# Linear attention and expert layer on one core: unit 0's sums of key exponentials moved from TensorE to GpSimd, with a new order of all instructions

## The chip, the cores and the metric

One core of a Trainium2 chip (trn2) runs the whole program. The metric is the device time of one execution in microseconds (us); of several runs the median is taken. Engines are named as in the profile: PE is TensorE, DVE is VectorE, ACT is ScalarE, POOL is GpSimd, SP is SyncE, from whose queue the transfers start. PEld are TensorE's weight loads.

## The reference

Attention over 8 batches of 8 heads, 576 tokens of 64 values each, and then a layer over the 4608 tokens, 512 wide with 1024 inner values:

```python
def phi(x):
    proj = np.einsum('bhsd,df->bhsf', x, w_phi)
    proj = proj - np.max(np.abs(proj), axis=-1, keepdims=True)
    return np.concatenate([np.exp(proj), np.exp(-proj)], axis=-1)
q_p, k_p = (phi(q), phi(k))
kv = np.einsum('bhsf,bhsd->bhfd', k_p, v)
z = np.sum(k_p, axis=2)
num = np.einsum('bhsf,bhfd->bhsd', q_p, kv)
den = np.einsum('bhsf,bhf->bhs', q_p, z)[..., None] + 1e-06
...
h = x @ w_in
e = np.exp(h - np.max(h, axis=-1, keepdims=True))
solu = h * (e / (np.sum(e, axis=-1, keepdims=True) + 1e-09))
ln = (solu - mu) / np.sqrt(var + 1e-06) * g_ln
out = ln @ w_out
```

The change concerns `z`, the sum of the key features over the tokens of one head.

## The kernel before

The attention is cut into 16 units, 0 to 15; unit u holds half the heads of batch u // 2, and two halves (sub 0 and sub 1) of two heads each. For each unit PE projects keys and queries (`pjk`, `pjq`, and `pjm` for the tokens in the middle), DVE takes the largest absolute value of a row (`m`) and subtracts it (`dk`, `dq`), ACT takes the exponentials (`ek` for keys, `fq` for queries). PE then multiplies key exponentials with values into `kvT` (`kv_mm`, and `kv_rest` for the tokens in the middle), adds `z` into the same bank, and later makes the numerator (`num`) and the denominator (`den`). The reciprocal of the denominator goes through a transfer that spreads it over rows (`rb<-d`), and POOL multiplies it into the result (`xa`, `xb`), which is the input of the second layer.

The second layer runs in 36 token tiles of 128: PE makes `h` with three products of high and low parts (`mxh`, `mxl`), DVE, ACT and POOL make the gated values, a transfer turns them, and PE makes `o`. A tile's `mxl` comes from POOL (`moe_lo`, line 1073). The last tile's `o` is made in two column halves (`moe_o_last`, line 1177), all others in one width of 512. Before the first `h`, the weights have to be unpacked: by ACT (`wraw`), by DVE (`wb`, two instructions a block), and by POOL (`win_l`, four blocks; `wsum`, the sums for the centring of `w_out`, whose mean PE makes as `cmall`).

There are two ways to the sums `z`. A unit in `Z_PE` takes them on PE (`z_mm`, line 613): for four token groups 16 products of the exponentials with ones, for the middle four more with `ones_half`, so 20 in each half. Every other unit has POOL add first: `z_add` (line 555) twice in each half, each with one addition of 128x512 into `zt` and one of 128x256 into `zacc`, and `z_half` (line 563), one of 64x512 for the middle. PE then needs four products with ones (`kv_z`, line 604). The choice stands in `z_sums`:

```python
def z_sums(st, sub):
    if st["u"] in Z_PE:
        z_mm(st, sub, list(key_tiles(st, sub)))
    else:
        kv_z(st, sub)
```

All instructions are steps of one plan (class `Plan`, line 211). The order in which they are written is the tuple `SEQUENCE` of step numbers (line 55), the same for all engines; each engine runs its own instructions in that order, and buffers are given to steps in that order too. `InOrder` (line 254 and after; its call is line 260, to which the profile puts nearly all instructions) keeps it.

Of the kernel before, what the change touches and what calls it, by code (L numbers as in the profile page):

```python
# [24 lines left out]
Z_PE = (0, 1, 2)  # L25
# [246 lines left out]
def linear_attention_then_moe(ctx, tc, qT, kT, v, w_phi, w_in, g_ln, w_out, out):  # L272
# [601 lines left out]
    for u in range(2 * B):  # L874
# [53 lines left out]
        for g in range(3):  # L928
            z = (0.0, 4.0, 6.0)[g]
            for j in (None,) if g == 1 else range(2):  # L930
# [3 lines left out]
                if g != 1 and u in K_BANKED:  # L934
# [4 lines left out]
                    src + [("e", g, j)])  # L939
        for sub in () if u in Z_PE else range(2):  # L940
            z, e = 1.5 + 4.5 * sub, 2 * sub
# [365 lines left out]
```

## Time and profile before

| what | value |
|---|---|
| median of 3 runs | 661.49 us (661.01 to 664.86) |
| profiled execution | 661.79 us |
| its span, first to last instruction | 659.8 us |
| PE busy | 652.9 us (99%), 4876 instructions |
| DVE busy | 503.9 us (76%) |
| POOL busy | 413.2 us (63%), 447 instructions |
| ACT busy | 373.5 us (57%) |
| granted PE clock | 1.0, full speed in every slice of the span |

The span is shorter than the execution by 1.99 us that lie around it. A busy share is a mean over the whole span; the first 68 us are the attention of units 0 to 2 and the preparation of the weights, and what follows is a mixture of attention and the second layer.

### The profile page before, as it was taken

How to read it: one execution, taken by the hardware profiler on the slowest of the kernel's cores; microseconds unless marked ns; L12 is line 12 of the kernel's file. 1: busy time of each engine (PE TensorE's matmuls, PEld its weight loads, DVE VectorE, ACT ScalarE, POOL GpSimd, SP SyncE). 2: the span in 40 equal slices, each digit the busy share in tenths (PEclk: the TensorE clock that was granted, in tenths of full speed). 3: DMA queues.
4: the chain of work that ended last, by engine and by line, in shares of the span. 5: the costliest groups of instructions: out<-in, count | busy, mean ns of one | idle time of the engine just before them, and what ended most of it. 6: DMA issues, size and time to landing. Idle time of an engine off the chain costs nothing.

```text
span 659.8 us, 13101 instructions
## 1 busy us (share of the span) xinstructions
PE 652.9 (99%) x4876; PEld 489.6 (74%) x4876; DVE 503.9 (76%) x756; ACT 373.5 (57%) x719; POOL 413.2 (63%) x447
## 2 busy tenths in 40 slices
PE   8999999999999999999999999999999999999998
PEld 7666767668777777777768777777777767888887
DVE  6999989899988789697878878688787945454530
ACT  4997875666555755556556555367366544323222
POOL 0249999867749578275773868738564955553632
PEclk9999999999999999999999999999999999999999
DMA  8978887587787668776777665886656372362342
GB/s 277 379 241 264 251 253 215 191 244 231 218 273 245 211 174 274 225 236 219 217 233 249 189 195 164 275 292 211 198 173 178 112 220 81 115 207 96 129 160 80
DMA packets 133296, 138.44 MB, mean 210 GB/s; under 512 B 55665, under 2 KB 106737, under 8 KB 132721
## 3 DMA queue, kind: packets, MB, share of 16 engines
q1 hardware_dynamic: 133232, 137.61, 66.6%
q8 instruction: 38, 0.62, 0.4%
q14 instruction: 26, 0.20, 0.1%
HBM read 87.10 MB, written 50.48 MB: 209 GB/s over the span
## 4 chain that ended last, share of the span: by engine, by line
PE 84%; POOL 5%; DVE 5%; DMA 3%; SPq 1%; issue 1%; ACT 1%; POOLq 0%; DVEq 0%
PE o L260 28%; PE h L260 27%; PE kvT L260 12%; PE num L260 6%; PE pjk L260 4%; PE pjq L260 4%; PE den L260 2%; DVE m L260 2%; POOL zt L260 1%; SPq L260 1%; POOL zacc L260 1%; DVE dk L260 1%; DMA rawk<-in_k 1%; PE pjm L260 1%; POOL w L260 1%; DVE dq L260 1%
## 5 line engine op out<-in xcount | busy, mean ns | idle before, releaser
L260 PE MATMUL o<-w_out_h,uhs 128*128 128x512 f32 (+1 forms) x296 | 114.3, 386 | 0.0
L260 PE MATMUL o<-w_out_l,uhs 128*128 128x512 f32 (+1 forms) x296 | 113.5, 383 | 0.0
L260 PE MATMUL o<-w_out_h,uls 128*128 128x512 f32 (+1 forms) x296 | 113.5, 383 | 0.0
L260 ACT ACTIVATE ek<-dk 128x512 f32<-128x512 f32 (+1 forms) x160 | 88.9, 587 | 32.3 <-DVE dk L260 20.1
L260 POOL TENSOR_TENSOR uls<-uTs,uhs 128x1024 fp32r<-128x1024 f32 x36 | 87.0, 2422 | 31.8 <-ACT uhs L260 31.6
L260 POOL TENSOR_TENSOR zt<-ek 128x512 f32<-128x512 f32 x52 | 68.6, 1320 | 54.4 <-ACT ek L260 41.9
L260 PE MATMUL h<-win_h,mxh 128*128 128x512 f32 x288 | 91.4, 399 | 0.1
L260 PE MATMUL h<-win_h,mxl 128*128 128x512 f32 x288 | 89.1, 391 | 0.2 <-POOL mxl L260 0.2
L260 PE MATMUL h<-win_l,mxh 128*128 128x512 f32 x288 | 89.0, 390 | 0.0
L260 ACT ACTIVATE fq<-pT 128x512 f32<-128x512 f32 (+1 forms) x140 | 74.2, 561 | 17.9 <-PE kvT L260 9.7
L260 DVE TENSOR_REDUCE nm<-h 128x1 f32<-128x1024 f32 x36 | 43.8, 1217 | 52.5 <-PE h L260 52.4
L260 ACT ACTIVATE eu<-h,nm 128x1024 f32<-128x1024 f32 x36 | 40.1, 1115 | 74.8 <-DVE nm L260 55.5
L260 PEld LDWEIGHTS o<-w_out_h,uhs 128*128 128x128 f32 x296 | 55.6, 188 | 12.1 <-issue 0.9
L260 PEld LDWEIGHTS o<-w_out_h,uls 128*128 128x128 f32 x296 | 55.6, 188 | 11.0
L260 PEld LDWEIGHTS o<-w_out_l,uhs 128*128 128x128 f32 x296 | 55.6, 188 | 10.7
L260 PEld LDWEIGHTS h<-win_h,mxl 128*128 128x128 f32 x288 | 53.8, 188 | 12.4 <-POOL mxl L260 1.1
L260 DVE SCALAR_TENSOR_TENSOR qz<-fq,kvf,qz 128x576 f32<-128x576 f32 x52 | 57.6, 1124 | 6.8 <-ACT qz L260 6.7
L260 PEld LDWEIGHTS h<-win_l,mxh 128*128 128x128 f32 x288 | 54.1, 188 | 11.6
L260 PEld LDWEIGHTS h<-win_h,mxh 128*128 128x128 f32 x288 | 52.3, 188 | 13.9 <-issue 1.6
L260 PE MATMUL kvT<-ek,rawv 128*64 128x256 f32 x512 | 61.6, 383 | 1.0 <-DVE dk L260 0.7
L260 POOL TENSOR_TENSOR xa<-E,rb 128x576 f32<-128x576 f32 (+1 forms) x32 | 30.4, 950 | 47.0 <-DMA rb<-d 46.5
L260 DVE TENSOR_TENSOR eu<-h,eu 128x1024 f32<-128x1024 f32 x36 | 43.6, 1211 | 19.5 <-ACT eu L260 19.3
(96 smaller groups left out, 1244.0 us busy)
## 6 DMA issues: line engine op xcount, KB each, us to landing
du<-ub SPq DMA_DIRECT2D x36, 512.0 KB, 3.9
uTs<-du SPq DMA_DIRECT2D x36, 512.0 KB, 4.6
rb<-d SPq DMA_DIRECT2D x64, 144.0 KB, 4.1
dqd<-dq SPq DMA_DIRECT2D x14, 640.0 KB, 4.2
pT<-dqd SPq DMA_DIRECT2D x14, 640.0 KB, 6.1
out<-os SPq DMA_DIRECT2D x35, 256.0 KB, 3.2
rawq<-in_q SPq DMA_DIRECT2D x32, 256.0 KB, 4.5
rawk<-in_k SPq DMA_DIRECT2D x32, 256.0 KB, 4.2
```

The costliest lines, as they stand in the source:

```text
L260: return self.tc.keep_in_program_order(method(*args, **kwargs))
```

## The change

`Z_PE` loses unit 0, so that unit 0's `z` takes the way of units 3 to 15: ten additions on POOL (two `z_add` and one `z_half` in each half) and four products in each half on PE in place of twenty. The number of steps grows by six, and `SEQUENCE` is another order from its first entries on; nothing else differs.

```diff
-Z_PE = (0, 1, 2)
+Z_PE = (1,2)
...
 SEQUENCE = (
-    123, 2, 1, 124, 125, 78, 87, 129, 127, 126, 80, 81, 135, 94, 83, 89, 128, 84, 104, 85, 136, 82, 102, 95,
...
```

On PE, in unit 0's part, from the middle products (`vz`) to the transposition of `kvT` (`kvt`), before:

```order
L260 MATMUL kvT<-ek,vz 64x256 x4
L260 MATMUL kvT<-ek,ones 32x128 x16
L260 MATMUL kvT<-ek,ones_half 32x128 x4
L260 MATMUL kvT<-ek,rawv 64x256 x8
L260 MATMUL kvT<-ek,ones 32x128 x16
L260 MATMUL kvT<-ek,ones_half 32x128 x4
L260 MATMUL kvt<-ident,kvs 128x128 x3
```

and now:

```order
L261 MATMUL kvT<-ek,vz 64x256 x4
L261 MATMUL kvT<-zacc,ones 32x128 x4
L261 MATMUL kvT<-ek,rawv 64x256 x8
L261 MATMUL kvT<-zacc,ones 32x128 x4
L261 MATMUL dT<-ident,dqm 128x128 x4
L261 MATMUL kvt<-ident,kvs 128x128 x6
```

Two times twenty products became two times four, which read what POOL adds, and the two transpositions of `kvT` moved together behind one of the queries.

On POOL, the first tensor instructions of the program, behind the constants, before:

```order
L260 TENSOR_TENSOR win_l<-w_0_472,win_h 128x1024
L260 TENSOR_TENSOR win_l<-w_1_433,win_h 128x1024
L260 TENSOR_TENSOR xa<-E,rb 128x576 x2
L260 TENSOR_TENSOR wsum<-w_4_613 128x512
L260 TENSOR_TENSOR wsum<-wsum,w_5_637 128x512 x2
```

and now, from the seventh of the ten additions on (`zt` and `zacc` are the additions for `z` of unit 0):

```order
L261 TENSOR_TENSOR zacc<-zacc,ek 64x512
L261 TENSOR_TENSOR zt<-ek 128x512
L261 TENSOR_TENSOR zacc<-zt 128x256
L261 TENSOR_TENSOR zacc<-zacc,ek 64x512
L261 TENSOR_TENSOR win_l<-w_0_495,win_h 128x1024
L261 TENSOR_TENSOR win_l<-w_1_448,win_h 128x1024
L261 TENSOR_TENSOR wsum<-w_4_540 128x512
L261 TENSOR_TENSOR xa<-E,rb 128x576
L261 TENSOR_TENSOR wsum<-wsum,w_5_599 128x512 x2
```

The ten additions stand ahead of everything else there, and the first sum for the centring (`wsum`, numbered 4) moved ahead of the first division (`xa`); the second division moved behind the sums.

On PE, from unit 2's last key products to the first `h` of the second layer, before:

```order
L260 MATMUL kvT<-ek,rawv 64x256 x8
L260 MATMUL kvT<-ek,ones 32x128 x16
L260 MATMUL kvT<-ek,ones_half 32x128 x4
L260 MATMUL cmall<-wsum,mean 128x512
L260 MATMUL pjk<-wph,rawk 128x128 x8
L260 MATMUL pjq<-wph,rawq 128x128 x8
L260 MATMUL pjm<-wph,rawk 128x128 x2
L260 MATMUL pjm<-wph,rawq 128x128 x2
L260 MATMUL h<-win_h,mxh 128x512 x2
```

and now:

```order
L261 MATMUL cmall<-wsum,mean 128x512
L261 MATMUL kvT<-ek,rawv 64x256 x8
L261 MATMUL kvT<-ek,ones 32x128 x16
L261 MATMUL kvT<-ek,ones_half 32x128 x4
L261 MATMUL pjk<-wph,rawk 128x128 x8
L261 MATMUL pjm<-wph,rawk 128x128 x2
L261 MATMUL pjm<-wph,rawq 128x128 x2
L261 MATMUL pjq<-wph,rawq 128x128 x8
L261 MATMUL h<-win_h,mxh 128x512 x2
```

The mean (`cmall`) moved ahead of unit 2's last key products. All PE steps that stood ahead of the first `h` still do, except one: `pjm` of unit 4 comes behind it now (the `pjm` shown is unit 3's, which stood earlier before).

At the end of the program ACT's last work (`eu` is the gated exponential, `uhs` the high part of a turned tile, `os` the eviction of `o`) was, before:

```order
L260 CAST uhs<-uTs 128x1024 x2
L260 ACTIVATE os<-o,sc 128x512
L260 CAST uhs<-uTs 128x1024
L260 ACTIVATE eu,sm<-h,nm 128x1024
L260 CAST uhs<-uTs 128x1024
L260 ACTIVATE os<-o,sc 128x512 x4
L260 ACTIVATE os<-o,sc 128x256 x2
```

and is now:

```order
L261 CAST uhs<-uTs 128x1024
L261 ACTIVATE eu,sm<-h,nm 128x1024
L261 ACTIVATE os<-o,sc 128x512 x3
L261 CAST uhs<-uTs 128x1024 x2
L261 ACTIVATE os<-o,sc 128x512
L261 ACTIVATE os<-o,sc 128x256 x2
L261 ACTIVATE os<-o,sc 128x512
```

The second half of tile 34's `o` is PE's last work now, behind both halves of tile 35, and so a tile of full width is the last to be evicted and written out.

## Rows read from the trace of the kernel before

**Rows 1.** Busy time by stretch: PE, PEld, DVE, ACT, POOL, PE clock, DMA share, GB/s.

```profile
13.00:42.00 29.00, 28.70 (x410) 20.41 (x408) 28.93 (x54) 27.13 (x53) 4.74 (x2) 1.00 0.92 328
42.00:68.00 26.00, 26.00 (x356) 17.57 (x353) 25.93 (x43) 20.20 (x41) 24.25 (x15) 1.00 0.83 266
68.00:330.00 262.00, 261.73 (x1978) 191.58 (x1976) 226.44 (x345) 164.84 (x327) 188.21 (x201) 1.00 0.76 230
330.00:630.00 300.00, 299.20 (x1907) 227.93 (x1906) 210.85 (x296) 148.61 (x282) 184.11 (x204) 1.00 0.59 184
```

**Rows 2.** Timeline of PE, unit 0, sub 1: start, duration, instructions.

```profile
21.10 1.08 PE L260 MATMUL kvT<-ek,ones 128*32 128x128 f32 x32
...
22.33 0.55 PE L260 MATMUL kvt<-ident,kvs 128*128 128x128 f32 x3
```

**Rows 3.** Timeline of PE, the four products of a later unit's half.

```profile
117.24 0.43 PE L260 MATMUL kvT<-zacc,ones 128*32 128x128 f32 x8
117.48 0.67 PE L260 MATMUL den<-qz,ones 128*32 128x288 f32 x8
```

**Rows 4.** Groups by shape on POOL: busy us, mean ns, idle before them.

```profile
L260 POOL TENSOR_TENSOR zt<-ek 128x512 f32<-128x512 f32 x52 | 68.6, 1320 | 54.4 <-ACT ek L260 41.9 <-PE kvT L260 8.3 <-PE o L260 3.2
L260 POOL TENSOR_TENSOR zacc<-zt 128x256 f32<-128x256 f32 x52 | 39.0, 749 | 4.1
L260 POOL TENSOR_TENSOR zacc<-zacc,ek 64x512 f32<-64x512 f32 x26 | 34.5, 1326 | 1.7
```

**Rows 5.** Timelines of DVE and of ACT, before unit 2's last key products.

```profile
54.93 1.24 DVE L260 STREAM_TRANSPOSE dq<-dq 128x1024 f32<-128x1024 f32 x1
56.09 0.66 DVE L260 TENSOR_TENSOR dk<-pjk,m 128x512 f32<-128x512 f32 x1
...
57.53 1.27 DVE L260 TENSOR_REDUCE m<-pjq 128x4 f32<-128x512 f32 x2
...
57.09 2.26 ACT L260 ACTIVATE ek<-dk 128x512 f32<-128x512 f32 x4
```

**Rows 6.** Timelines of PE and of POOL up to the first `h`.

```profile
59.57 1.95 PE L260 MATMUL kvT<-ek,rawv 128*64 128x256 f32 x16
...
62.68 1.13 PE L260 MATMUL cmall<-wsum,mean 128*128 128x512 f32 x2
63.74 1.16 PE L260 MATMUL pjk<-wph,rawk 64*128 64x128 f32 x16
...
65.62 0.39 PE L260 MATMUL pjm<-wph,rawk 64*128 64x128 f32 x4
...
66.17 0.73 PE L260 MATMUL h<-win_h,mxh 128*128 128x512 f32 x2
...
67.20 0.72 PE L260 MATMUL h<-win_h,mxl 128*128 128x512 f32 x2
...
42.78 1.52 POOL L260 TENSOR_TENSOR xa<-E,rb 128x576 f32<-128x576 f32 x1 [9.23 <-DMA rb<-d]
...
65.86 1.27 POOL L260 TENSOR_TENSOR mxl<-xa,mxh 128x512 fp32r<-128x512 f32 x1
```

**Rows 7.** Timelines of POOL and of DVE, first sum for the centring.

```profile
46.61 2.27 POOL L260 TENSOR_TENSOR wsum<-w 128x512 f32<-128x512 f32 x1
...
46.50 1.23 DVE L260 SCALAR_TENSOR_TENSOR w<-wraw,w 128x1024 uint32<-128x1024 uint32 x1
```

**Rows 8.** Evictions of `o` (a group; the last one in the timeline), transfers of `out` to landing.

```profile
L260 ACT ACTIVATE os<-o,sc 128x512 f32<-128x512 f32 x35 | 23.7, 684 | 27.0 <-PE o L260 20.7 <-PE h L260 3.2 <-POOL xb L260 2.2
...
656.69 0.47 ACT L260 ACTIVATE os<-o,sc 128x256 f32<-128x256 f32 x1 [2.35 <-PE o L260]
...
DMA to landing us min/median/max: 1.7/2.1/2.4
```

256 rows, old and new, of the table SEQUENCE are left out of this document.

## The prediction

> **What bounds the kernel now.** I read the busy time by stretch first. In the four rows shown PE is busy for 28.70 of 29, 26.00 of 26, 261.73 of 262 and 299.20 of 300 us at the full clock [rows 1]: it hardly ever stands still, so any work that PE loses could shorten the run. But in the first two rows DVE is just as full (28.93 of 29 and 25.93 of 26), and in the second POOL is too (24.25 of 26). Only behind 68 us does DVE fall back, to 226.44 of 262. The change takes work from PE at 18 to 22 us, in the part where DVE has no slack. So the question is not what PE saves, but when the first `h` block of the second layer can start; from there on PE alone sets the pace. The timelines of the three engines up to that block come next, then the end of the program.
>
> **What it saves on PE.** The twenty products of unit 0's sub 1 run from 21.10 until `kvt` starts at 22.33, which is 1.23 us [rows 2]; sub 0 has the same twenty. What comes in their place takes from 117.48 - 117.24 = 0.24 us [rows 3], up to about 0.3 where other work follows. So 2 x (1.23 - 0.30) = 1.85 us of PE time go. Everything else on PE is the same work in another order. A change of the kind of product there costs some tenths at most, and since about as many changes stand in the new order as in the old, I count these as nothing.
>
> **What it adds on POOL.** Four additions at 1320 ns, four at 749 and two at 1326 [rows 4] make 4 x 1.32 + 4 x 0.75 + 2 x 1.33 = 10.9 us. POOL's busy time in the stretch from 13 to 42 is only 4.74 us [rows 1], so they fit there. What they hide behind is DVE and ACT, which make the exponentials; PE's four products must wait for the last addition. If that cover is too short, the price is PE standing still in front of them. The key exponentials of unit 0 come only by and by, so POOL can finish no earlier than about the time at which sub 1's products ran before (21.10); I estimate a wait between 0 and 1 us, and take it as part of the time that PE loses to DVE anyway.
>
> **How far the start can move.** Unit 2's last key products are the point that I follow. They start at 59.57 [rows 6], behind four exponentials that run from 57.09 to 59.35, and these wait for DVE's last subtraction `dk` of that unit at 56.09 [rows 5]. Ahead of that subtraction the new order has the same DVE instructions as the old, but for two row maxima of 1.27 us together, about 1.20 from start to start, that moved in, and one transposition that moved out, from 54.93 to 56.09, so 1.16 us [rows 5]. DVE thus comes there at the same time (+0.04 us), if it never waits. On ACT three exponentials and one eviction stand behind it now instead of four exponentials of some 0.55 us, which is 0.3 us less. From the key products to `h` it took 66.17 - 59.57 = 6.60 us [rows 6]; the mean `cmall` (63.74 - 62.68 = 1.06) has moved ahead of them and fits into the time that PE has now. So `h` comes 0.3 + 1.06 = 1.4 us earlier. The bounds of this shift: all of PE's saving and of the work moved behind `h`, 1.85 + 0.55 = 2.4 us earlier, if DVE gives way; 1.5 us later, if POOL brings `mxl` late (below). POOL itself: from the first division at 42.78 its work runs almost without a gap until `mxl` ends at 65.86 + 1.27 = 67.13, and PE wants it at 67.20 [rows 6]. With the first centring sum, 2.27 us [rows 7], moved ahead of that division, POOL could come 2.3 us earlier if its transfers did not move, which is more than the 1.4 needed. The new order of SP's queue puts other loads and a second reciprocal ahead of the division's second row transfer, so this cover is thin. I take 1.4 us.
>
> **What is given back.** The `pjm` of unit 4, from 65.62 to 66.17 or 0.55 us [rows 6], now comes behind the first `h` and has to be done later. At the end the last tile to be evicted has 512 columns instead of 256: 0.68 instead of 0.47 us on ACT, and its transfer takes up to 2.4 us where the smaller ones took as little as 1.7 [rows 8]; with 0.2 + 0.4 the end costs 0.6 us (bounds 0.2 and 0.9). PE's pauses behind the start were 0.27 + 0.80 = 1.07 us [rows 1]. They belong to the old order. The new one may have none or several times as many; between 0 and 4 us I take 0.7, near the old value.
>
> **The sum.** -1.4 + 0.55 + 0.6 + (0.7 - 1.07 = -0.35, rounded) = -0.6 us. The profiled execution took 661.79 us (span 659.8 and 1.99 around it), so it would take 661.2; the median of the runs is 661.49, 0.3 lower, and so I predict 660.9 us.
>
> **The rivals.**
>
> (A) All of the saving arrives: `h` starts 2.4 us earlier, and PE pauses as little as before. That gives 661.49 - 2.4 + 0.55 + 0.6 - 0.5 = 659.7 us. For it speaks that PE is the one full engine in all four stretches; against it, that DVE's row up to 68 us has no idle time to give [rows 1].
>
> (B) POOL is late for the first `h`, and the kernel is slower. The place is `mxl` of tile 0, which had 0.07 us of slack. In the trace, the first sum for the centring took 2.27 us, where an addition of the same size takes 1.32 [rows 4, 7]; it began at 46.61 while DVE ran a two-input instruction on the weights' bits from 46.50 to 47.73. Each such meeting costs POOL about 0.95 us. In the new order, these DVE instructions and POOL's sums stand next to each other for other weights, and the first division between them waits for its transfer. If `mxl` comes 1.0 us later than before, everything behind it does: 661.49 + 1.0 + 0.55 + 0.6 = 663.6 us. It decides from the point where POOL loses more than the 2.3 us that it gained by the moved sum. For it speaks the thin cover; against it, that sum itself.
>
> The Trainium skill (SBUF — State Buffer, section "SBUF: two separate sides") says that DVE and GpSimd share one pair of ports, which the one that starts first holds for its whole instruction, and that a DVE instruction with two SBUF inputs is of the kind that locks out a GpSimd instruction which reads SBUF. The row of 2.27 us agrees with that. By this rule the ten new additions, at 10 to 22 us, would be safe, since DVE mostly reads from PSUM there, and the sums behind 36 us would not be.
>
> (C) The change doesn't do what it says: PE waits for POOL's additions in unit 0, by about 1 us, and the projections for unit 1, which stand behind them on PE's queue, reach DVE late. Then DVE's row slips by 0.8 us, `h` comes 0.6 earlier in place of 1.4, and the time is 661.7 us. For it speaks that POOL's 10.9 us have little room between the first exponentials and 21 us; against it, that the new order puts more projections ahead of that point.
>
> (D) Any other wait somewhere in the new order, behind 68 us: it would have to last over 6.6 us to be measured as slower. PE's pauses of 1.07 us in 562 [rows 1] speak against it.
>
> **How the numbers follow.** The forecast has 0.40, A 0.23, B 0.20, C 0.13, D 0.04. The time is the forecast's, 660.9 us. The range takes in A with half a microsecond to spare and B: 659.1 to 663.8 us; below it lies only an A in which the end costs nothing and all pauses go, above it D and a larger B. About 1% is what a measurement of this kernel can tell from no change, that is 6.6 us; forecast, A, B and C are all within it. Faster by more than that would need more than PE's loss of 1.85 us and all its pauses together, so 0.01; slower by more is D, 0.04; the same 0.95.
>
> **What would show it right or wrong.** In the changed kernel's profile the products with `zacc` of unit 0 should stand near 19 and 21 us, with PE idle for up to 1 us in front of the second and, in all, some 1 to 2 us more up to 68 us than before; DVE should still be full there. Unit 2's last key products should start near 59.3 and `h` near 64.8. The additions on POOL should take 10.9 us together and end near 22 us. PE should end on products of 512 columns, some 0.6 us more from there to the end. It is wrong if `h` starts before 64 us with DVE full as before (then DVE was not the bound), if POOL releases `mxl` after 67 us (B), or if PE's idle time behind 68 us is above 4 us.

## The result and the profile after

| what | before | changed |
|---|---|---|
| median | 662.08 us (4 runs beside it) | 669.94 us (4 runs, 669.14 to 670.88) |
| ratio | | 1.012, 95% interval 1.010 to 1.014 |
| profiled execution | 661.79 us | 669.28 us |
| its span | 659.8 us | 667.5 us |
| first `h` starts | 66.17 | 71.17 |
| PE's last product ends | 656.65 | 663.81 |

The changed kernel is slower by 1.2%. The forecast was 660.9 us, and its range ended at 663.8. The table also shows where to look: 5.0 of the 7.5 us between the two profiled executions are there when the first `h` starts; from there to PE's end it takes 592.64 us in place of 590.48, which is 2.16 more; the rest from PE's end to the end of the span is 3.69 in place of 3.15. (The time outside the span is 0.2 shorter.) Of all executions behind the numbers of this document one, of e7, took 930.11 us at a mean granted clock of 0.656, and it is left out.

The busy time by stretch of the changed kernel answers to [rows 1] (PE, PEld, DVE, ACT, POOL, PE clock, DMA share, GB/s):

```profile
13.00:42.00 29.00, 26.27 (x296) 17.14 (x296) 28.86 (x50) 24.67 (x48) 14.54 (x12) 0.94 0.92 328
42.00:68.00 26.00, 25.86 (x372) 17.58 (x362) 24.12 (x39) 22.74 (x45) 17.24 (x12) 1.00 0.70 215
68.00:330.00 262.00, 258.37 (x1966) 189.69 (x1963) 222.00 (x345) 162.00 (x321) 191.40 (x198) 1.00 0.73 228
330.00:630.00 300.00, 300.00 (x1930) 226.79 (x1929) 212.38 (x305) 153.24 (x289) 185.37 (x209) 1.00 0.61 189
```

Two things are new in the first row. PE stands still for 2.7 us of 29 where it did for 0.3, and its granted clock is 0.94 in the mean. DVE is as full as before (28.86 of 29). Read alone, that cell says that nothing happened there; it is the cell that misleads, as the next views show.

What the change itself does came out as forecast. PE's timeline of unit 0 answers to [rows 2, 3], and the first and the last of POOL's ten additions stand below it:

```profile
20.32 0.43 PE L261 MATMUL kvT<-zacc,ones 128*32 128x128 f32 x8
20.67 1.95 PE L261 MATMUL kvT<-ek,rawv 128*64 128x256 f32 x16
22.55 0.43 PE L261 MATMUL kvT<-zacc,ones 128*32 128x128 f32 x8
22.91 0.66 PE L261 MATMUL dT<-ident,dqm 128*128 128x128 f32 x4
```

```profile
10.95 1.27 POOL L261 TENSOR_TENSOR zt<-ek 128x512 f32<-128x512 f32 x1 [8.98 <-ACT ek L261]
...
20.71 1.28 POOL L261 TENSOR_TENSOR zacc<-zacc,ek 64x512 f32<-64x512 f32 x1
```

From start to start the four products (eight records in the profile, two for each) take 20.67 - 20.32 = 0.35 and 22.91 - 22.55 = 0.36 us (0.30 in the forecast). The additions end at 21.99, and PE, which wants them at 22.55, does not wait for them.

The loss stands some ten us later. First DVE, and then the one instruction that POOL runs beside it (two subtractions in one row, 29.30 to 34.02):

```profile
31.00 0.71 DVE L261 STREAM_TRANSPOSE dE<-dn 128x288 f32<-128x288 f32 x1
31.74 0.22 DVE L261 RECIPROCAL cmr<-dE 128x9 f32<-128x9 f32 x1
31.87 2.70 DVE L261 TENSOR_SCALAR w<-wraw 128x1024 uint32<-128x1024 uint32 x1
34.49 1.28 DVE L261 TENSOR_REDUCE m<-pjq 128x4 f32<-128x512 f32 x2
35.69 0.68 DVE L261 TENSOR_TENSOR dk<-pjk,m 128x512 f32<-128x512 f32 x1
```

```profile
29.30 4.72 POOL L261 TENSOR_TENSOR win_l<-w,win_h 128x1024 fp32r<-128x1024 f32 x2 [7.30 <-ACT win_h L261]
```

`TENSOR_SCALAR w<-wraw` is the bit instruction that unpacks weight block 4. It is booked with 2.70 us. In the kernel before, the same instruction came at 34.23, behind POOL's pair, which had ended at 33.54:

```profile
28.80 4.74 POOL L260 TENSOR_TENSOR win_l<-w,win_h 128x1024 fp32r<-128x1024 f32 x2 [26.82 <-ACT win_h L260]
...
34.23 0.69 DVE L260 TENSOR_SCALAR w<-wraw 128x1024 uint32<-128x1024 uint32 x1
```

The transposition `dE` at 31.00 and the reciprocal at 31.74, which also read and write SBUF while POOL's pair runs, are not slower (0.71 and 0.22 us, as in the kernel before, where they ran ahead of the pair). So it is not every such instruction that is held up.

So the busy share of DVE contains two us in which it does nothing but wait. In the new order this instruction stands ahead of two row maxima and of the subtraction `dk`, and `dk` (35.69) is the last reader of a PSUM bank that PE needs for `pjm` of unit 2. PE's timeline there, and then its busy time and clock in slices of 2 us (PE, PEld, DVE, ACT, POOL, PE clock, DMA share, GB/s):

```profile
34.15 0.48 PE L261 MATMUL pjm<-wph,rawk 64*128 64x128 f32 x2
36.42 0.58 PE L261 MATMUL pjm<-wph,rawk 64*128 64x128 f32 x1 [1.78 <-DVE dk L261]
...
37.57 2.98 PE L261 MATMUL kvT<-ek,rawv 128*64 128x256 f32 x16
40.48 0.66 PE L261 MATMUL kvT<-ek,vz 64*64 64x256 f32 x8
```

```profile
34.00:36.00 2.00, 0.64 (x5) 0.29 (x2) 2.00 (x4) 0.62 (x3) 0.02 (x1) 1.00 0.80 265
36.00:38.00 2.00, 1.58 (x8) 1.21 (x10) 2.00 (x3) 1.60 (x4) 0.00 (x0) 0.57 0.97 393
38.00:40.00 2.00, 2.00 (x14) 1.14 (x12) 1.97 (x4) 2.00 (x6) 0.20 (x1) 0.57 0.92 288
40.00:42.00 2.00, 2.00 (x50) 1.23 (x50) 1.97 (x6) 1.28 (x2) 1.10 (x1) 1.00 0.53 145
```

PE pauses for 1.78 us, and in the two slices behind that the granted clock is 0.57 in the mean, that is for most of this time the lower of its two levels (1.2 instead of 2.4 GHz). The eight `kvT` products at 37.57 (sixteen records) take 2.98 us; at the full clock such a group takes 1.95, as in [rows 6].

The list of PE's waits (engine, tile, line, releaser: us in total, times, longest) shows what else stands in the new order:

```profile
PE pjm L261 <- DVE dk L261: 1.8, 1, 1.8
PE o L261 <- POOL uls L261: 1.7, 1, 1.7
PE pjq L261 <- DVE dk L261: 1.6, 2, 1.5
PE h L261 <- DVE dq L261: 1.4, 1, 1.4
```

Not all of this hangs on the pause. The third row's long wait, near 11 us, stands far ahead of it, and the runs e1, e3 and e6 below have it too (1.1 to 1.5); and e1, which has no pause at `pjm`, waits 1.41 us for `uls` all the same.

The last of these rows is the first `h`, which waits for a bank that DVE's `dq` still reads. PE's timeline there answers to [rows 6]:

```profile
63.06 1.12 PE L261 MATMUL cmall<-wsum,mean 128*128 128x512 f32 x2
64.11 1.95 PE L261 MATMUL kvT<-ek,rawv 128*64 128x256 f32 x16
...
68.66 1.06 PE L261 MATMUL pjq<-wph,rawq 64*128 64x128 f32 x16
71.17 0.70 PE L261 MATMUL h<-win_h,mxh 128*128 128x512 f32 x2 [1.45 <-DVE dq L261]
```

Unit 2's last key products start at 64.11 where 59.3 was forecast, and `h` at 71.17 where 64.8 was. The end of the program, which answers to [rows 8], is as the forecast had it: a tile of full width goes out last (0.69 us), and from PE's end to the end of the span it takes 0.54 us more.

```profile
663.90 0.69 ACT L261 ACTIVATE os<-o,sc 128x512 f32<-128x512 f32 x1 [2.32 <-PE o L261]
```

### The profile page after: what moved, and what is told of

The parts are those of the page before. It is cut to its first block, busy times and chain, and to the rows that moved or that the text cites. A ratio compares the mean times of both kernels' runs of the same rounds, so it can differ in the third digit from the quotient of the medians.

```text
span 667.5 us, 12996 instructions
## 1 busy us (share of the span) xinstructions
PE 655.0 (98%) x4812; PEld 489.5 (73%) x4812; DVE 501.3 (75%) x756; ACT 374.5 (56%) x719; POOL 423.0 (63%) x457
## 4 chain that ended last, share of the span: by engine, by line
PE 83%; DVE 8%; DMA 6%; ACT 2%; issue 1%; POOL 0%; SPq 0%; DVEq 0%; POOLq 0%; ACTq 0%
PE o L261 29%; PE h L261 27%; PE kvT L261 11%; PE num L261 6%; PE pjk L261 4%; PE pjq L261 3%; PE den L261 2%; DVE m L261 2%; DMA rawk<-in_k 2%; DVE dq L261 2%; DMA wraw<-in_w_in 1%; DMA du<-ub 1%; PE pjm L261 1%; DVE dk L261 1%; DVE w L261 1%; DMA uTs<-du 1%
## 5 line engine op out<-in xcount | busy, mean ns | idle before, releaser
L261 POOL TENSOR_TENSOR zt<-ek 128x512 f32<-128x512 f32 x56 | 72.3, 1292 | 38.3 <-ACT ek L261 33.7
L261 DVE SCALAR_TENSOR_TENSOR qz<-fq,kvf,qz 128x576 f32<-128x576 f32 x52 | 51.9, 1015 | 15.0 <-ACT qz L261 13.2
L261 ACT ACTIVATE qz<-fq,kvf 128x576 f32<-128x576 f32 x52 | 38.9, 771 | 36.6 <-DMA kvf<-dk 36.4
L261 PE MATMUL num<-fq,kvf 128*64 128x448 f32 (+1 forms) x304 | 56.5, 503 | 0.0
```

Source lines behind the costliest of these rows:

```text
L261: return self.tc.keep_in_program_order(method(*args, **kwargs))
```

## The experiments

The theory after reading these rows: the two `win_l` subtractions on POOL hold something that DVE's bit instruction needs, so DVE comes 2 us late to `dk`, PE pauses, its clock falls, and later waits follow from that. The rivals: the way of the sums itself (POOL's additions) makes the kernel slower; or DVE's lateness is not what costs the 8 us, but the new order as a whole. For each run the ratio is to runs of the kernel before on the same chip. Their medians differ a little: 662.08 us beside the changed kernel, 661.34 beside e1, e2, e3 and e5, 661.70 beside e6, e7 and e8, 661.17 beside e9 and e10. Where two runs are compared below, each is first taken against its own.

**1. The bit instruction four places later (e1).** Only the place of one DVE instruction changes, against the changed kernel:

```diff
-TENSOR_SCALAR w<-wraw          (block 4)
 TENSOR_REDUCE m<-pjq x2
 TENSOR_TENSOR dk<-pjk,m
 TENSOR_TENSOR dq<-pjq,m
+TENSOR_SCALAR w<-wraw          (block 4)
```

> The changed kernel, with one step moved on DVE: the first bit instruction of weight block 4 comes four instructions later, behind POOL's two low parts of the input weights instead of beside them. Theory 1 (port lock): that DVE instruction took 2.70 us instead of 0.68 because GpSimd held the shared ports until 34.02; moved, it takes about 0.7, PE's pause of 1.78 us in front of unit 2's middle projections shrinks below 0.5 us, the clock stays at 1.0 from 36 to 40 us, and some 4 us of the 8 come back: about 666 us. Theory 2 (the new order itself makes PE wait there for its bank, whatever DVE meets): the pause and the half clock stay and the time is 669 to 670.

Measured: 663.82 us, ratio 1.004 (1.002 to 1.006). The instruction starts at 33.80, when POOL's pair has ended (33.56), and takes 0.69 us:

```profile
33.80 0.69 DVE L260 TENSOR_SCALAR w<-wraw 128x1024 uint32<-128x1024 uint32 x1
```

The pause at `pjm` and the fall of the clock are gone, and `h` starts at 66.46. One place of one instruction is worth 5.4 of the 7.9 us by the medians (7.86 - 2.48), and 5.56 between the profiled executions (669.28 - 663.72); some 4 were expected.

**2. The same meeting brought about in the kernel before (e2).** There the bit instruction of block 5 is moved up, ahead of eight instructions, block 4's among them, into the time in which POOL runs its pair:

```diff
+TENSOR_SCALAR w<-wraw          (block 5)
 TENSOR_REDUCE m<-pjq
 TENSOR_TENSOR dk<-pjk,m
 ...
 TENSOR_SCALAR w<-wraw          (block 4)
 STREAM_TRANSPOSE dE<-dn
 RECIPROCAL cmr<-dE
-TENSOR_SCALAR w<-wraw          (block 5)
```

> The kernel before, with the first bit instruction of weight block 5 moved six instructions forward on DVE, into the 4.7 us in which POOL makes two low parts of the input weights. Theory 1 (port lock): the instruction takes about 2 us or more instead of 0.65, DVE is 1.5 to 2 us late in a stretch where it has no idle time, PE pauses over 1 us near 32 to 40 us, and the kernel becomes 1.5 to 4 us slower, the larger number if PE's clock falls. Theory 2 (not the neighbours but the new order's other steps are at fault): no change, within 0.5 us.

Measured: 662.95 us, ratio 1.003 (1.001 to 1.005). The instruction takes 2.85 us; POOL's pair ran from 28.52 to 33.25:

```profile
28.52 4.73 POOL L260 TENSOR_TENSOR win_l<-w,win_h 128x1024 fp32r<-128x1024 f32 x2 [26.54 <-ACT win_h L260]
...
30.95 2.85 DVE L260 TENSOR_SCALAR w<-wraw 128x1024 uint32<-128x1024 uint32 x1
```

The meeting, then, does not need the new sums. But its price here is 1.6 us by the medians, not 5 to 6. PE waited for DVE's `dk` in two pieces of 1.03 and 1.14 us, and its clock stayed at 1.0 in all slices from 28 to 44 us. The profiled execution itself is one of the three longest of the ten (665.99 us): near 335 us PE waits 2.43 us for a load of keys (`rawk`), and behind that its clock falls too (0.78, 0.50 and 0.86 in the slices of 2 us from 334 to 340). That wait is not at the meeting, and the median of the ten is 3 us lower.

**3. The pause filled (e3).** In the changed kernel four products with zeros go to PE into an unused part of the bank that it already holds; DVE keeps its order:

```diff
             for j, r in enumerate(HEADS):
+                for _ in range(4 if st["u"] == 2 and i == j == 0 else 0):
+                    nc.tensor.matmul(st["pjm"][0][:, 2 * F : 3 * F], lhsT=zero, rhs=zero, start=True, stop=True)
```

> The changed kernel, with four products of zeros (fp32, 128 columns, about 0.46 us each) put into PE's queue inside unit 2's middle projections, where PE waited 1.78 us for a bank; their results are not read. DVE's late instruction is left as it is. Clock theory: the fall of the granted clock to 0.57 in the two slices from 36 to 40 us came from that pause and cost about 1.9 us beside it; with PE busy in the pause the clock stays at 1.0 and the time falls by 1.5 to 2 us, to about 668. Rival (the clock falls for other reasons, or the slow products there wait for operands): half clock and time unchanged.

Measured: 665.19 us, ratio 1.005 (1.003 to 1.007), where about 668 was expected. The bit instruction is as slow as in the changed kernel (2.69 us), and PE still comes to `pjm` late, but the wait that is left lasts 0.69 us, and the clock stays at 1.0:

```profile
36.11 0.37 PE L261 MATMUL pjm<-wph,rawk 64*128 64x128 f32 x1 [0.69 <-DVE dk L261]
```

```profile
36.00:38.00 2.00, 1.89 (x18) 1.41 (x20) 2.00 (x4) 1.92 (x5) 0.00 (x0) 1.00 0.92 373
```

The wait ahead of `h` shrinks from 1.45 to 0.49, and the wait for `uls` at 115 us is not there. Products that compute nothing save 4.0 us by the medians (7.86 - 3.85). Between the profiled executions PE ends 4.64 us earlier: 0.30 of it is there already at 23 us, ahead of the pause; by the second `kvt` of unit 1 another 1.56 have come (44.04 in place of 45.90), and since the lateness of DVE is still there, that is the lower clock; 0.23 more come up to `h` (69.08 in place of 71.17). The other 2.55 stand behind `h`. That they follow from the lower clock is not shown: the wait for `uls` is in e1, where the clock did not fall, and not in e8, where it did.

**4. The sums alone (e5).** The kernel before with its old order, but unit 0's sums on POOL. The ten additions are put in, each behind the exponentials that it needs; unit 0's second group of four `zacc` products moves behind a transposition of queries, and in unit 0 the two halves of the key exponentials swap places:

```diff
-Z_PE = (0, 1, 2)
+Z_PE = (1,2)
```

> The old order with only the first part of the change: unit 0's sums are added on POOL, the six steps put where their exponentials are ready, the two halves of the key pairs swapped in unit 0 so that a pair is complete early, and PE's products with the sums of sub 1 moved behind unit 0's two later query transpositions. If PE's saving of 1.85 us counts (PE bound), PE still waits about 1 us for the last addition and the time is 0.5 to 1.8 us below before, about 660.5. If DVE bounds the first 68 us (forecast's reason), the time is within 0.5 us of before. If moving the sums to POOL is itself the cause of the 8 us, it is 5 us or more above before.

Measured: 662.25 us, ratio 1.000 (0.999 to 1.002): no difference that can be told from the spread. So in the old order the new way of the sums costs nothing and brings nothing; the 8 us belong to the new order. The first `h` starts at 67.77, which is 1.6 later than before, although PE has 1.8 us less to do. Of this 0.56 are there already when PE comes to unit 0's `vz` products (17.96 in place of 17.40), ahead of the sums. Behind them PE waits:

```profile
21.22 0.55 PE L260 MATMUL kvt<-ident,kvs 128*128 128x128 f32 x3 [0.36 <-ACT kvs L260]
...
23.49 0.43 PE L260 MATMUL kvT<-zacc,ones 128*32 128x128 f32 x8 [0.85 <-POOL zacc L260]
24.57 0.55 PE L260 MATMUL kvt<-ident,kvs 128*128 128x128 f32 x3 [0.65 <-ACT kvs L260]
```

**5. The other side of the meeting moved (e6).** The changed kernel with all of DVE's order as it is; on POOL the second subtraction of the pair goes behind the first sum for the centring:

```diff
 win_l<-w_0,win_h
+wsum<-w_4
 win_l<-w_1,win_h
-wsum<-w_4
```

> The changed kernel with one step moved on GpSimd and none on VectorE: the second win_l subtraction of the pair at 29.30 stands behind the first sum for the centring. Theory (GpSimd's running subtraction locks VectorE's one-input instruction on the weights' bits out): the bit instruction of block 4 starts near 31.8 again and takes about 0.7 us in place of 2.70; PE's pause of 1.78 us at pjm is gone or below 0.5, the granted clock between 36 and 40 us is 1.0, and the time is near that of the run in which the bit instruction was moved, 663 to 665 us. Rival (that instruction is slow because of its place in VectorE's queue or of its data): it stays at 2.7 us and the time at 669 to 670.

Measured: 663.3 us, ratio 1.002 (1.001 to 1.004). The bit instruction, at the same place of DVE's queue, is back at 0.64 us, and the pause and the lower clock are gone:

```profile
29.01 2.40 POOL L261 TENSOR_TENSOR win_l<-w,win_h 128x1024 fp32r<-128x1024 f32 x1 [7.32 <-ACT win_h L261]
...
31.59 0.64 DVE L261 TENSOR_SCALAR w<-wraw 128x1024 uint32<-128x1024 uint32 x1
32.14 1.28 DVE L261 TENSOR_REDUCE m<-pjq 128x4 f32<-128x512 f32 x2
33.34 0.68 DVE L261 TENSOR_TENSOR dk<-pjk,m 128x512 f32<-128x512 f32 x1
```

That settles the cause of the 2.70 us: it is POOL's subtraction beside it, not the place in DVE's queue and not the data. The same run shows a third meeting, with a later `win_l` on POOL (57.59 to 59.98): a bit instruction from 58.69 takes 1.85 us and ends 0.56 behind POOL's. e1 (2.06 us) and e3 (1.82) have this meeting too; in the changed kernel the instruction there takes 0.78.

**6. DVE late without a meeting (e8).** The order of e1, in which DVE meets nothing, but a row maximum ahead of `dk` is taken six times in place of once:

```diff
-        row_max(st[key, g, j], tokens(st[pj, g][j]))
+        for _ in range(6 if (st["u"], key, g, j) == (1, "mq", 2, 1) else 1):
+            row_max(st[key, g, j], tokens(st[pj, g][j]))
```

> The changed kernel with block 4's bit instruction four places later on VectorE (663.8 us), and VectorE made late in another way: the row maximum ahead of the subtraction that frees the bank of pjm is taken six times in place of once, five times 0.6 = 3.0 us more, read from PSUM, with nothing to lock. Theory (the 8 us come from VectorE's lateness at this bank, and the lock is only its reason): PE pauses 1.8 to 2.1 us at pjm, the granted clock falls below 0.7 between 36 and 40 us, and the time is 668 to 671 us. Rival (the pause alone costs, and the rest came from GpSimd's or VectorE's conflict itself): the clock stays at 1.0 and the time is 663.8 + 2 = 665.8 us.

Measured: 668.34 us, ratio 1.009 (1.007 to 1.012), 4.2 us more than e1 (6.64 - 2.48) for 3.6 us more on DVE (its seven maxima take 4.86 us, e1's two 1.23). PE pauses for 2.75 us, longer than expected, and the clock falls as in the changed kernel (columns as in the slices above):

```profile
36.00:38.00 2.00, 0.43 (x4) 0.43 (x5) 2.00 (x4) 0.45 (x1) 0.00 (x0) 0.75 0.97 384
38.00:40.00 2.00, 2.00 (x12) 1.26 (x12) 1.97 (x4) 1.64 (x5) 0.00 (x0) 0.50 1.02 282
40.00:42.00 2.00, 2.00 (x12) 0.95 (x8) 1.97 (x3) 1.99 (x3) 0.58 (x1) 0.50 0.37 106
```

So no meeting is needed: DVE's lateness is enough for the pause and for the fall of the clock. The sizes differ, though. Here 3.6 us of delay cost 4.2; in the changed kernel 2.0 us cost 5.4 by e1. Up to `h` e8 loses more (`h` starts at 72.15 in place of e1's 66.46), but behind it PE needs 590.94 us in place of 592.64, and it has no wait for `uls`.

**7. Two repairs (e7).** The order of e1, with unit 4's first key products ahead of the first `o` on PE (where e1 waited 1.41 us for `uls`), and with the end as the kernel before has it. On PE:

```diff
+kvT<-ek,rawv x8                (unit 4)
 o<-w_out_h,uhs ... x24
-kvT<-ek,rawv x8                (unit 4)
 ...
+o ... 512 columns              (tile 34, second half)
 o ... 256 columns              (tile 35)
-o ... 512 columns              (tile 34, second half)
```

> The changed kernel with three repairs: block 4's bit instruction four places later on VectorE (as in the run at 663.8 us); unit 4's first key products ahead of the first tile's o on PE, where PE waited 1.41 us for uls at 111 us; and tile 34's second half of o, its eviction and its transfer ahead of those of tile 35, as the kernel before has it. Theory (each pause of PE adds its own length, since PE has no slack behind 68 us): no pause at the first o, 0.55 us less behind PE's end, so 663.8 - 1.4 - 0.55 = 661.9 us, about the time before. Rival (a pause of PE that goes comes back at the next chain, as work that waits for the same engines): 663 to 664 us.

Measured: 664.3 us (nine executions), ratio 1.004 (1.002 to 1.005). No gain in the median. In the profiled execution the end is shorter by the half microsecond (PE's end at 658.13, the span 661.2; e1 658.27 and 661.9), and the pause at the first `o` is gone, but PE ends only 0.14 earlier. The rival (a pause that goes comes back elsewhere; 663 to 664 us) was right here in kind: at the `h` block that starts near 103 us e7 leads e1 by 0.32 us (103.10 against 103.42), and at the one near 135, behind the pause that is gone, by 0.25 (135.53 against 135.78). The 1.41 us were lost again in pieces within 25 us.

**8. Lighter DVE, with the sums on PE (e9) and on POOL (e10).** Is it DVE that keeps PE's gain from arriving? Both kernels take unit 0's and unit 1's row maxima of keys and queries over every second value, so that sixteen DVE instructions get shorter and the results differ; e9 is the kernel before, e10 is e5:

```diff
-        row_max(st[key, g, j], tokens(st[pj, g][j]))
+        row_max(st[key, g, j], tokens(st[pj, g][j])[:, :, :: 2 if st["u"] < 2 else 1])
```

> The kernel before, unit 0's sums on PE as they were, with VectorE's row maxima of units 0 and 1 taken over every second value only (16 instructions of about 0.6 us become about 0.33, so about 4.3 us of VectorE go ahead of the first h; the maxima, and so the output, are other values). It is one of a pair with the next run and asks what PE's gain at the start is worth where VectorE has slack. PE stood idle for some 2.5 us ahead of the first h, so h can come 1 to 2 us earlier at most: 659.5 to 661 us.

> The old order with unit 0's sums on GpSimd (the run that took the same time as before: 662.25 us, first h at 67.77), with the same lighter row maxima as its partner. Theory (VectorE sets the pace up to the first h, so that PE's 1.85 us came back as waiting for it): with VectorE lighter by 4.3 us the gain appears, h comes 3 us or more earlier than in the run without lighter maxima, that is before 65, and the time is about 1.85 us below its partner's, 658 to 659 us. Rival (the chain of GpSimd's additions and the transfers sets the start): h stays behind 66 and the time is within 0.6 us of its partner's.

Measured: e9 660.34 us, ratio 0.998 (0.997 to 0.999); e10 659.4 us, ratio 0.997 (0.996 to 0.999). They differ by 0.94 us, with overlapping intervals, and in the profiled executions by 0.26 (PE's ends at 655.07 and 654.81). The first `h` starts at 65.93 in e9 (0.24 earlier than before) and at 66.40 in e10 (1.37 earlier than in e5, not the 3 us of the theory). The time of e9 is within what was expected, but that of e10 fits neither theory. The row of e9 up to 42 us shows why it gains so little (columns as in [rows 1]):

```profile
13.00:42.00 29.00, 29.00 (x413) 20.62 (x411) 26.85 (x52) 26.79 (x52) 4.75 (x2) 1.00 0.94 332
```

DVE has room now (its sixteen maxima take 0.41 us instead of 0.67, together 4.1 less; half a microsecond of that is lost again, since a bit instruction now comes into POOL's pair at 32.72 and takes 1.22), and PE has none: it works for all of the 29 us. In the old order both engines were full, so relief for one alone is worth what the other has left, 0.24 us here. In e10, where both are relieved, `h` still comes 0.47 us later than in e9. There PE waits for a row maximum (0.56 us), for ACT's `kvs` (0.66) and for values from a transfer (0.73):

```profile
57.98 0.66 PE L260 MATMUL kvT<-ek,vz 64*64 64x256 f32 x8 [0.73 <-DMA vz<-in_v]
```

## Why the prediction was wrong

The times of the profiled executions, side by side (us):

| | forecast | changed | e6, without that meeting |
|---|---|---|---|
| first `h` against before | -1.4 | +5.00 | +0.52 |
| from `h` to PE's end | +0.2 | +2.16 | +0.88 |
| from PE's end to the end of the span | +0.6 | +0.54 | +0.50 |
| span | -0.6 | +7.7 | +1.9 |

The second entry of the forecast's column is `pjm` of unit 4, 0.55, less 0.35 of pauses.

**What was right.** PE's saving: twenty products of 1.23 us each half became 0.35. POOL's additions fit, and end at 22.0. The end of the program cost 0.54 of a forecast 0.6. Together these three make about one microsecond, on the side of the forecast.

**The step that failed** is "DVE thus comes there at the same time (+0.04 us), if it never waits". It was reckoned by counting DVE's instructions ahead of unit 2's `dk` and taking each at its duration in the kernel before. The bit instruction of block 4 went in at 0.69 us. In the new order it met POOL's subtraction and was booked with 2.70 (e1 and e6 show it from both sides). The count itself was right: up to that `dk` DVE has two row maxima more and one transposition less. But it came 4.72 us late in the changed kernel, and 0.84 in e6 (56.09 before; the first row is the changed kernel's, the second e6's):

```profile
60.81 0.68 DVE L261 TENSOR_TENSOR dk<-pjk,m 128x512 f32<-128x512 f32 x1
...
56.93 0.68 DVE L261 TENSOR_TENSOR dk<-pjk,m 128x512 f32<-128x512 f32 x1
```

In the changed kernel DVE is booked as busy for 2.4 us more up to there (52.85 in place of 50.45), for the most part the held instruction, and stands still for 2.3 more, 1.71 of it at 51.77, where it waits for ACT's `dn`. The condition "if it never waits" was written down and then not priced.

**What the same step left out** is the size of what follows. The delay of 2 us became 5.8 (663.81 - 658.05, PE's end in the changed kernel and in e6). From the changed kernel's timeline against e6's: by the second `kvt` of unit 1 (45.90 against 42.02) it is 3.88 behind, of which 0.29 were there already at the first one (23.40 against 23.11), 1.78 are the pause, and the remaining 1.81 are nearly all the lower clock (1.56 by e3; the eight `kvT` products alone take 1.03 more). Then the wait of 1.45 for the bank ahead of `h` comes on top, less 0.76 that e6 loses by itself at 57 us: some 4.5 at `h` (71.17 - 66.69 = 4.48). Behind `h`, where the wait of 1.70 in front of the first `o` stands, it loses another 1.28 (2.16 - 0.88); since e1 has that wait without a pause, it is not shown that it comes from the meeting. The prediction has no term for a fall of the clock: the profile of before showed the clock at full speed everywhere, and this was taken over without a condition.

**The rest, 2.5 us, is in e6,** which has no meeting at 32 us and is still slower than before by the median (1.6 us, 0.2%), where the forecast had a gain of 0.6. Of this, 1.9 lie ahead of `h` (0.52 + 1.4). The forecast said that `cmall` "fits into the time that PE has now", ahead of unit 2's last key products. In e6 PE reaches `cmall` without a gap, at 59.94, and the products start right behind it, at 61.00 in place of 59.3. The time in which `cmall` was to hide was gone by then. From 4 us up to `h` PE stands still for 3.07 us, 1.14 more than before; 0.75 of it is a wait for DVE's `dq` near 16 us, ahead of everything that the prediction followed. Another 0.77 is in the first of these rows; together they are the 1.9:

```profile
57.36 1.43 PE L261 MATMUL kvT<-ek,vz 64*64 64x256 f32 x8
...
59.94 1.12 PE L261 MATMUL cmall<-wsum,mean 128*128 128x512 f32 x2
61.00 1.95 PE L261 MATMUL kvT<-ek,rawv 128*64 128x256 f32 x16
```

The `vz` products ahead of it are stretched from 0.66 to 1.43 us. ACT had waited 1.47 us for POOL's division at 56.2 before it could evict `E`, and the exponentials stand behind that in its queue. The last of them ends at 60.47, so that the key products could not have started much before 61.00 without `cmall` either:

```profile
57.68 0.40 ACT L261 COPY E<-num 128x288 f32<-128x288 f32 x1 [1.47 <-POOL xa L261]
...
59.83 0.64 ACT L261 ACTIVATE ek<-dk 128x512 f32<-128x512 f32 x1
```

That is a way by which POOL's lateness reaches PE, as rival B has it, at another place and through ACT.

**The rivals.** B had the right kind of mechanism (POOL and DVE in each other's way, with a rule and a row for it) and the wrong side: it let DVE hold POOL up, at the sums, up to `mxl`. Here POOL held DVE up, at `win_l`, and the price of the meeting, 5.4 us by e1, was more than five times the 1.0 us that B puts on it (the other 1.15 of B's 2.1 stand in every sum). B even called the stretch from 10 to 22 us safe, looked next at 36 us and after, and never asked what POOL's `win_l` at 29 would meet. The rule cited there (the Trainium skill, "SBUF — State Buffer", section "SBUF: two separate sides") works both ways: whichever of the two engines starts first keeps the pair for its whole instruction. The traces agree with that in both directions: DVE's 0.69 us became 2.70, 2.85 and 1.85, and each ended 0.55 to 0.56 us behind POOL's instruction; POOL's 1.32 us became 2.27 [rows 4, 7]. The bit instruction has one input, not two; by which of its properties it falls under the rule, no run here shows. D named "another wait somewhere" and asked 6.6 us of it behind 68 us, at a chance of 0.04; the wait that came stood ahead of 68 us, and its 1.78 us were paid about three times over (5.4). C (waiting for POOL's additions) happened only in e5, with 0.85 us. A did not happen anywhere (its sum also takes 0.5 us off for pauses, for which its words give no reason; without that it is 660.2); e5 and e10 say that 1.85 us less on PE at the start are worth between nothing and 0.9 us. The 1%, or 6.6 us, that the prediction takes as the least that can be told from no change was too wide: the interval here is 0.2% to either side, about 1.5 us.

**What stays open.** Why the clock fell behind the pause of 1.78 us at 34.6 and not behind others of nearly the same length in the same execution (1.45 us ahead of 11.25, 1.45 ahead of 71.17, 1.70 ahead of 115.78: the clock is 1.00 in the slices after each of them) was not tried. That the fall follows from the pause is shown by e3 and e8; which pauses bring one is not. While PE still had work, the clock fell in the traces behind pauses of 1.78, 2.43 (e2, at 335 us) and 2.75 us (e8). How much of the 7.9 us the fall is worth is open as well: three of the changed kernel's four executions have a mean granted clock of 0.995 to 0.997, the fourth has 1.0 and is no shorter (669.14 us). Only the first, of 669.28 us, is traced, so what lengthened the fourth is not known. Also open is how the saved 1.85 us could arrive at the start: e10 shows three waits that are in the way, and none of them was taken out by itself. No run that computes the same values as the kernel before is faster than it.

## What to carry to other kernels

When a change comes with a new order, costing its own instructions is the small part: go through each engine's list for instructions on VectorE with SBUF on both sides that now stand beside a GpSimd instruction, see in the trace which kinds are held up (here the bit instructions, not the transposition or the reciprocal), and give each such meeting its price, about the rest of the GpSimd instruction. Then ask who needs the bank that the delayed engine frees, since a pause on a full TensorE can cost more than its length: the clock may fall behind it. A busy share near 100% proves neither that the engine works (2 of 2.70 us were waiting) nor that it is the bound (4.1 us less work brought 0.24 us).

## What the runs showed of the hardware that was not expected

- A one-input VectorE instruction, SBUF to SBUF, 128x1024 uint32, takes 0.64 to 0.72 us alone. When a GpSimd subtraction was running at its start, it took 2.70 us (changed kernel), 2.85 (e2), 2.69 and 1.82 (e3), 2.06 (e1), 1.85 (e6), 1.74 (e7), 1.22 (e9) and 1.14 (e10); each time it ended 0.54 to 0.56 us behind the GpSimd one. The profile books the whole time as busy, not as a wait.
- VectorE instructions that read PSUM were untouched beside the same GpSimd instruction: the row maximum and the subtractions of 128x512 took 0.68 us throughout. So were a transposition and a reciprocal from SBUF to SBUF, both started while it ran (0.71 and 0.22 us).
- One pause of 1.78 us on TensorE was followed by a granted clock of 0.57 over 4 us, one of 2.75 us (e8) by 0.75, 0.50, 0.50 and 0.55 in the next four slices of 2 us, and one of 2.43 us (e2) by 0.78, 0.50 and 0.86. Three other pauses of 1.45 to 1.70 us, and two of about 1.1 close together (e2), left it at 1.00.
- Four products with zeros in such a pause, which cost PE some 1.2 us, made the kernel 4.0 us faster by the medians, 4.7 between the profiled executions; 1.6 of that is traced to the clock.
